# Short column ranges and full-width last row blocks in the small products of a linear-attention gradient

## The chip, the cores and the metric

The kernel runs on one core of a Trainium2 chip. A core has TensorE (matrix products; PE in the profile, PEld for the loading of its stationary operand), VectorE (DVE), ScalarE (ACT), GpSimd (POOL) and SyncE (SP, which here only issues transfers), an on-chip memory of 128 partitions (SBUF), and eight accumulation banks (PSUM) that TensorE writes and VectorE and ScalarE read. Transfers between memories (DMA) are issued on the queues of SP, ACT and POOL.

The metric is the device time of one execution in microseconds (us). The kernel before took 1066.45 us, the median of three runs (1065.12, 1066.45, 1068.38).

## The reference

Two attention blocks are computed, forward and backward, on 2048 tokens of width 448 with 16 heads of 28 columns. Block A is linear attention, block B is softmax attention with one shared key and value head. The program returns the output and the gradients of both inputs and of all weights.

```python
# block A (x: 2048 x 448, wqkv: 448 x 1344, wo: 448 x 448)
q, k, v = heads of x @ wqkv                      # 16 heads of 28 columns
phi = lambda t: where(t > 0, t + 1, exp(t)) + 1e-6
pq, pk = phi(q), phi(k)
kv  = einsum("bhsd,bhse->bhde", pk, v)           # one 28 x 28 matrix per head
z   = einsum("bhsd->bhd", pk)
num = einsum("bhqd,bhde->bhqe", pq, kv)
den = einsum("bhqd,bhd->bhq", pq, z) + 1e-6
a   = concat_heads(num / den) @ wo
# block B: softmax((x wq)(x wk)^T / sqrt(28)) (x wv), then @ wo
# result: [a, b] and the vector-Jacobian product with grad_out for all eight inputs
```

What matters for this document is `kv`. Laid out for all heads at once it is a 448 x 448 matrix in which only 16 blocks of 28 x 28 on the diagonal are not zero. Its transpose, its gradient and the transpose of that have the same shape.

## The kernel before

The work has two halves. Block A and the preparation of block B (`phase_A`, `phase_B_pre`) come first and take about 218 us. Then one loop over 512 steps computes the softmax attention of block B and its gradients, in an order that is written out by hand (`tc.manual_schedule()`). The change lies in the first half only. There, a scheduler in the framework puts each engine's instructions in order at build time; each engine then runs its own list in that order, and waits between engines are semaphores. Every transfer on the SP and ACT queues also uses one of eight completion semaphores in turn, so that its issue waits until the transfer that had the same semaphore before has landed.

Matrices of width 448 are held as four chunks of 128, 128, 128 and 64 rows (`DC_ROWS`, line 19). A product with 448 output rows is thus done in four row blocks `i`, each summing over four chunks `k` of the contraction. `HR` (line 22) gives for each chunk the columns in which a block-diagonal matrix is not zero: 140, 168, 140 and 84 columns, where neighbours overlap by 28 because heads straddle the chunk borders.

These parts of block A are touched, in their order of execution:

- `blkprod` (lines 285 to 297) makes a block-diagonal matrix: for each row block it multiplies only the columns of `HR[i]` and masks the result on VectorE (line 297). It is used four times: for the transpose of kv (line 333), for kv (line 336), for the transpose of its gradient (line 428) and for its gradient (line 453). Each has 32 products, 8 of them in the last row block.
- `prod_to` (lines 299 to 306) makes a product of two 448 x 448 matrices, one of them block-diagonal. With `full=False` the block-diagonal one is the stationary operand and only the chunks that are not zero are summed (`chunks_of`): KO (line 341) and VWT (line 451), 10 products each. With `full=True` the block-diagonal one is the moving operand, and all its 448 columns are streamed for each of 16 products: KOT (line 339) and VW (line 429). The result is copied out of PSUM by whichever of ScalarE and VectorE the scheduler picks (line 306).
- The last loop of weight gradients (lines 457 to 477) makes, for each row block `i`, two results. The first is K1, held in two parts of bfloat16, times the gradient of kv, which is block-diagonal: 8 products of 448 columns (line 463). The second is kv times the two parts of G: 4 or 6 products of 512 columns (line 473). ScalarE copies each result into a tile `osb` (lines 466 and 476) and issues its store (lines 467 and 477). There are three `osb` tiles and four PSUM tiles named `agen`.

All of these products go through `mm` (line 80), so that their line in the profile is L81. In the last row block, `i = 3`, the stationary operand has 64 columns instead of 128.

Around these parts stand large products on the same engine: `st1`, `st3`, `outA` and the sums into `gacc` (lines 347 to 388), the weight gradients `gw` (lines 409 to 426, called on lines 430 and 504), the loop that makes `gkn` (lines 431 to 437) and the loop that makes the input gradient (lines 509 to 516).

Of the kernel before, what the change touches and what calls it, by code (L numbers as in the profile page):

```python
# [11 lines left out]
BF16 = mybir.dt.bfloat16  # L12
# [4 lines left out]
D = 448  # L17
P = 128
# [3 lines left out]
HR = [(0, 140), (112, 280), (252, 392), (364, 448)]  # L22
# [3 lines left out]
def kernel(  # L26
# [21 lines left out]
    nc = tc.nc  # L48
# [31 lines left out]
    def mm(out_ap, lhsT, rhs, start=True, stop=True):  # L80
        nc.tensor.matmul(out_ap, lhsT=lhsT, rhs=rhs, start=start, stop=stop, tile_position=(0, 0))  # L81
# [23 lines left out]
    def w_T(t, w, off, r3=0):  # L105
        for cc in range(4):
            r = DC_ROWS[cc]
            r0 = r3 if cc == 3 else 0
            nc.sync.dma_start_transpose(t[:, :, cc * P:cc * P + r], w[r0:r0 + r, cc, off:off + 512])
        return t  # L110
# [6 lines left out]
    def chunks_of(i):  # L117
        lo, hi = HR[i]
        return [k for k in range(4) if k * P < hi and k * P + DC_ROWS[k] > lo]

    def cs(i):
        return slice(i * P, i * P + DC_ROWS[i])

    def phase_A(pa, cA, cB, awk, psA):
# [11 lines left out]
        w3 = R3  # L136
# [24 lines left out]
        woA = cA.tile([P, 4, 512], BF16, name="woA")  # L161
# [33 lines left out]
        def mask(i):  # L195
            lo, hi = HR[i]
            return blkm[:, i, :, :].rearrange("p h e -> p (h e)")[0:DC_ROWS[i], 0:hi - lo]

        K1T = [ppB[:, 8 + 4 * i:12 + 4 * i, :] for i in range(2)]
        K1 = [cA.tile([P, 4, 4, P], BF16, name=f"K1{i}") for i in range(2)]  # L200
        kv_blk, kvT_blk, KO, KOT = (cA.tile([P, 4, D], BF16, name=n) for n in ("kv", "kvT", "KO", "KOT"))
        dkv_blk = R4[:, :, 0:D]
        dkvT_blk, VW, VWT = kvT_blk, KOT, KO
        zrow = cA.tile([P, D], BF16, name="zrow")
# [9 lines left out]
        for t in (KO, KOT):  # L214
            nc.gpsimd.memset(t[64:128, 3, :], 0.0)
        zero = [t[:, c, :] for t in (kvT_blk, kv_blk, dkv_blk) for c in range(4)]
        wvT = w_T(cA.tile([P, 4, D], BF16, name="wvT"), w3, 2 * D)
        woT = w_T(cA.tile([P, 4, D], BF16, name="woT"), woA, 0)

        def xT(st):  # L220
            ps = gen([P, 4, P], BF16)
# [63 lines left out]
        def blkprod(dst, lhs, rhs, name="agen"):  # L285
            for i in range(4):
                lo, hi = HR[i]
                r = DC_ROWS[i]
                ps = psA.tile([P, D], F32, name=name)
                ops = [(l_, r_) for l_ in lhs for r_ in rhs]  # L290
                n = len(ops) * 4
                k = 0
                for l_, r_ in ops:
                    for c in range(4):
                        mm(ps[0:r, 0:hi - lo], l_(c, i)[:, 0:r], r_(c)[:, lo:hi], start=(k == 0), stop=(k == n - 1))
                        k += 1
                nc.vector.tensor_tensor(out=dst[0:r, i, lo:hi], in0=ps[0:r, 0:hi - lo], in1=mask(i), op=ALU.mult)

        def prod_to(dst, lhs, rhs, full):
            for i in range(4):  # L300
                r = DC_ROWS[i]
                ps = gen([P, D])
                ks = range(4) if full else chunks_of(i)
                for n, k in enumerate(ks):
                    mm(ps[0:r, :], lhs[:, k, cs(i)], rhs[:, k, 0:D], start=(n == 0), stop=(n == len(ks) - 1))
                nc.any.tensor_copy(out=dst[0:r, i, :], in_=ps[0:r, :])

        def den(q4):
# [81 lines left out]
        GT = [gaB[:, 4 * i:4 * i + 4, :] for i in range(2)]  # L390
        G = [v4(ga[:, 4 * i:4 * i + 4, :]) for i in range(2)]
# [33 lines left out]
                g_ = nc.gpsimd.dma_start(out_2[c * P:c * P + r, blk * D:(blk + 1) * D], sb[0:r, :])  # L425
            return g_

        blkprod(dkvT_blk, [lambda c, i: woT[:, c, cs(i)]], [lambda c: GT[0][:, c, 0:D], lambda c: GT[1][:, c, 0:D]])
        prod_to(VW, wvT, dkvT_blk, True)
        gw(gqn, 0)  # L430
        for st in range(NS):
            ps = gen([P, D])
# [17 lines left out]
            nc.sync.dma_start(wo_pr[32 * j + 1:32 * j + 1 + DH, g, 0:D], B_wo[h * DH:(h + 1) * DH, :])  # L450
        prod_to(VWT, dkvT_blk, wvT, False)
        nc.gpsimd.dma_start(VWT[64:128, 3, :], wqT[0:64, 3, :])
        blkprod(dkv_blk, [lambda c, i: GT[0][:, c, cs(i)], lambda c, i: GT[1][:, c, cs(i)]], [lambda c: woT[:, c, :]])
        gkT = v4(gaB)
        for q4 in range(4):
            dma_T(gkT, gkn, 4 * q4, 4)
        for i in range(4):
            r = DC_ROWS[i]
            ps = gen([P, D])
            n = 0  # L460
            for j in range(2):
                for k in range(4):
                    mm(ps[0:r, :], K1[j][:, i, k, 0:r], dkv_blk[:, k, :], start=(n == 0), stop=(n == 7))
                    n += 1
            sb = awk.tile([P, 512], BF16, name="osb")[:, 0:D]
            nc.scalar.activation(out=sb[0:r, :], in_=ps[0:r, :], func=ACT.Copy)
            nc.scalar.dma_start(out_2[i * P:i * P + r, 2 * D:3 * D], sb[0:r, :])
            ps = gen([P, 512])
            ks = chunks_of(i)
            n = 0  # L470
            for j in range(2):
                for k in ks:
                    mm(ps[0:r, :], kv_blk[:, k, cs(i)], G[j][:, :, k, :], start=(n == 0), stop=(n == 2 * len(ks) - 1))
                    n += 1
            sb = awk.tile([P, 512], BF16, name="osb")[:, 0:D]
            nc.scalar.activation(out=sb[0:r, :], in_=ps[0:r, 0:D], func=ACT.Copy)
            nc.scalar.dma_start(out_3[i * P:i * P + r, :], sb[0:r, :])
# [31 lines left out]
        for st in range(NS):  # L509
            ps = gen([P, D])  # L510
            n = 0
# [607 lines left out]
```

## Time and profile before

| | |
|---|---|
| median of the runs | 1066.45 us (1065.12 to 1068.38) |
| span of the profiled execution | 1064.7 us |
| TensorE busy | 1023.1 us, 96%, 16241 products |
| VectorE, ScalarE, GpSimd busy | 899.5, 870.4, 780.7 us |
| first product of the hand-ordered loop | 217.9 us after the start |
| KOT, start of its products to start of the next | 52.99 to 56.23 us |
| VW, the same | 105.97 to 109.21 us |
| last loop of weight gradients | 135.19 to 145.79 us |

The span runs from the first to the last instruction; the page gives no other time for the profiled execution, and the three runs lie 0.4 to 3.7 us above the span. Busy time of TensorE counts a product from its start to its modelled end, and products overlap, so that the distance between starts is what one costs in a row of them. A line of the timeline gives start, length, engine, source line, operation, the tile written and the tiles read, the shape, the count, and in brackets the idle time before it with what ended it. A line of the chain gives start, length and what the program's end is traced back to.

### The profile page before, as it was taken

What the parts mean: (1) busy time and instruction counts of PE and PEld (TensorE: products, weight loads), DVE (VectorE), ACT (ScalarE), POOL (GpSimd) and SP (SyncE); (2) the same over time, 40 slices, a digit from 0 to 9 for tenths busy, and PEclk for the clock granted to TensorE, in tenths of its full rate; (3) what the DMA queues carried; (4) which work ended last, traced back from release to release, by engine and by line L of the source; (5) the groups of instructions that cost most, each with busy time, mean ns of one, the idle gap of its engine ahead of it and who ended that gap; (6) DMA issues with size and microseconds to landing.
All of it is one profiled execution on the core that took longest, in us unless ns stands there. A gap on an engine that the chain in (4) does not pass through costs nothing.

```text
span 1064.7 us, 40036 instructions
## 1 busy us (share of the span) xinstructions
PE 1023.1 (96%) x16241; PEld 489.1 (46%) x16241; DVE 899.5 (84%) x1797; ACT 870.4 (82%) x1741; POOL 780.7 (73%) x1033
## 2 busy tenths in 40 slices
PE   9999999998999999999999999999999999999998
PEld 5555455434444444444444444444444444444444
DVE  7887400459999999999999999999999999999942
ACT  6463222489999999999999999999999999999522
POOL 6001242218888898899889989988998999888881
PEclk9999999999999999999999999999999999999999
DMA  9849899079999999999999999999999999999963
GB/s 264 167 108 192 171 203 246 22 137 181 193 188 196 182 203 189 188 202 191 197 181 197 181 196 195 193 189 194 196 197 192 199 190 183 208 190 177 222 141 89
DMA packets 689937, 195.15 MB, mean 183 GB/s; under 512 B 670616, under 2 KB 687792, under 8 KB 689752
## 3 DMA queue, kind: packets, MB, share of 16 engines
q1 hardware_dynamic: 680152, 179.92, 99.6%
q0 software_dynamic: 4640, 8.71, 2.9%
q10 hardware_dynamic: 4960, 3.96, 1.3%
q8 instruction: 127, 2.08, 0.8%
q14 instruction: 58, 0.48, 0.2%
HBM read 12.60 MB, written 10.84 MB: 22 GB/s over the span
## 4 chain that ended last, share of the span: by engine, by line
PE 43%; ACT 32%; issue 14%; POOL 5%; DVE 4%; DMA 1%; ACTq 0%; DVEq 0%; POOLq 0%
ACT cp L938 16%; PE agen L81 14%; ACT eT L970 13%; PE agen L656 10%; PE aacc L656 10%; PE aacc L81 5%; POOL dsT L939 3%; PE aacc L790 2%; ACT eT L924 2%; PE aacc L821 1%; DVE dsT L936 1%; DVE dsx L1003 1%; DMA out_dram<-dsT 1%; POOL eT L754 1%; POOL out_dram L778 0%
## 5 line engine op out<-in xcount | busy, mean ns | idle before, releaser
L939 POOL TENSOR_TENSOR dsT<-cp,eT 128x512 bf16<-128x512 bf16 x512 | 587.9, 1156 | 78.9 <-ACT cp L938 71.7
L1003 DVE STREAM_TRANSPOSE dsx<-dsT 128x512 f32<-128x512 f32 x512 | 357.6, 699 | 2.9 <-POOL dsT L939 0.8
L656 PEld LDWEIGHTS <-R 32*128 32x128 bf16 (+1 forms) x9104 | 227.9, 94 | 274.1 <-issue 238.4
L936 DVE TENSOR_TENSOR dsT<-agen,eT 128x512 bf16<-128x512 f32 x512 | 341.7, 667 | 10.9 <-PE agen L656 5.6
L938 ACT ACTIVATE cp<-agen 128x512 bf16<-128x512 f32 x512 | 315.8, 617 | 12.3 <-PE agen L656 11.2
L924 ACT ACTIVATE eT<-aacc 128x512 bf16<-128x512 f32 x512 | 313.6, 612 | 14.8 <-PE agen L656 4.8
L970 ACT ACTIVATE eT<-aacc 128x512 bf16<-128x512 f32 x512 | 322.2, 629 | 0.0
L656 PE MATMUL agen<-dsx,qX 32*32 32x512 bf16 x4096 | 267.6, 375 | 0.0
L656 PE MATMUL agen<-doT,R 32*128 32x256 bf16 x2048 | 247.1, 269 | 3.4 <-DVE dsT L936 1.4
L656 PE MATMUL aacc<-R,R 32*128 32x256 bf16 (+1 forms) x2240 | 218.2, 268 | 7.2 <-DVE oTs L800 2.5
L656 PE MATMUL agen<-eT,R 128*32 128x256 bf16 x2048 | 157.5, 274 | 0.1
L656 PE MATMUL agen<-dsT,R 128*32 128x256 bf16 x2048 | 156.8, 274 | 0.1
L656 PEld LDWEIGHTS <-qX 32*32 32x32 bf16 x4096 | 79.8, 89 | 113.7 <-issue 53.3
L656 PE MATMUL aacc<-eN,don 128*32 128x512 bf16 x1024 | 97.1, 379 | 0.1
L81 PEld LDWEIGHTS <-R 128*128 128x128 bf16 (+1 forms) x517 | 40.8, 98 | 43.5 <-issue 11.5
L406 POOL COPY pk<-R 128x256 bf16<-128x256 bf16 x4 | 1.6, 397 | 73.8 <-DVE R L366 73.7
L81 PE MATMUL agen<-R,R 128*128 128x448 bf16 (+1 forms) x180 | 42.1, 361 | 0.6 <-ACT R L225 0.6
L832 POOL COPY qst<-R 128x512 bf16<-128x512 bf16 x56 | 34.2, 611 | 4.0 <-DMA qX<-qst 3.9
L656 PEld LDWEIGHTS <-don 128*32 128x32 bf16 x1024 | 33.8, 97 | 1.4 <-issue 1.0
L804 POOL TENSOR_TENSOR prod<-R,oTs 128x128 f32<-128x128 bf16 x64 | 27.6, 431 | 9.3 <-DVE oTs L800 9.3
L422 DVE TENSOR_TENSOR osb<-aacc,pr 64x448 bf16<-64x448 f32 x2 | 1.2, 618 | 38.3 <-DMA out_dram<-osb 24.4
L955 DVE TENSOR_SCALAR R<-agen 64x256 bf16<-64x256 f32 x64 | 27.3, 427 | 3.6 <-PE agen L656 1.6
(231 smaller groups left out, 967.8 us busy)
## 6 DMA issues: line engine op xcount, KB each, us to landing
out_dram<-osb ACTq DMA_DIRECT2D x22, 112.0 KB
eN<-eT SPq DMA_TRANSPOSE x128
xa<-in_A_x_dram SPq DMA_DIRECT2D x8, 224.0 KB
ga<-in_grad_out_dram SPq DMA_DIRECT2D x4, 448.0 KB
xa<-in_grad_out_dram POOLq DMA_DIRECT2D x4, 448.0 KB, 6.1
out_dram<-wdq POOLq DMA_DIRECT2D x8, 224.0 KB, 4.0
eT<-in_grad_out_dram SPq DMA_DIRECT2D x4, 448.0 KB
eT<-in_B_x_dram SPq DMA_DIRECT2D x4, 448.0 KB
```

The costliest lines, as they stand in the source:

```text
L81: nc.tensor.matmul(out_ap, lhsT=lhsT, rhs=rhs, start=start, stop=stop, tile_position=(0, 0))
L656: nc.tensor.matmul(out, lhsT=lhsT, rhs=rhs, start=start, stop=stop, tile_position=pos, skip_group_check=True)
L790: nc.tensor.transpose(onp[:, qb, :, :].rearrange("p h c -> p (h c)"), oTs[0:64, qb * P:(qb + 1) * P], identF[0:64, 0:64], tile_position=(0 ...
L804: nc.gpsimd.tensor_tensor(out=prod[b][:], in0=dnv, in1=os_, op=ALU.mult)
L832: eng.tensor_copy(out=st.rearrange("p (b s) a j -> p b s a j", s=2)[:, :, s, :, :], in_=src.unsqueeze(2).to_broadcast([P, 4, 4, 32]))
L924: nc.scalar.activation(out=eT(u)[:, 0, :], in_=sp[0][:, :], func=ACT.Exp, scale=scale)
L936: nc.vector.tensor_tensor(out=dst[:, 0, :], in0=dp[0][:, :], in1=ew[:, 0, :], op=ALU.mult)
L938: nc.scalar.activation(out=cp[:, :], in_=dp[1][:, :], func=ACT.Copy)
L939: nc.gpsimd.tensor_tensor(out=dst[:, 1, :], in0=cp[:, :], in1=ew[:, 1, :], op=ALU.mult)
L955: nc.vector.tensor_scalar(out=qT_B[g][64 * hp:64 * hp + 64, qc * 256:(qc + 1) * 256], in0=oq[64:128, 0:256], scalar1=scale, scalar2=None, ...
L970: nc.scalar.activation(out=eT(u)[:, 1, :], in_=sp[1][:, :], func=ACT.Exp, scale=scale)
L1003: nc.vector.transpose(out=dsx[b][:, tp, :, :, :].rearrange("p h t c -> p (h t c)").bitcast(F32), in_=dsT[y][:, :, :].rearrange("p h c -> p ...
```

## The change

Three things are edited.

First, the products whose moving operand is block-diagonal stream, for each chunk, only the columns of `HR`. This holds for KOT and VW (`prod_to` with `full=True`) and for K1 times the gradient of kv. A new helper, `by_heads`, issues them: 140, 168, 140 or 84 columns each, written to the same columns of one PSUM bank; only the first product of a group starts the sum.

Second, the last row block is computed 128 rows wide in all of these products, with 128 stationary columns; rows 64 to 127 of the result are not read.

Third, to have 64 more columns to read behind the last chunk, `wvT`, `woT`, `kv_blk` and `kvT_blk` become parts of one tile `blks` with 64 zero columns at its end; `cols` gives a row block of 128 columns that runs on into the chunk behind it.

```diff
-        kv_blk, kvT_blk, KO, KOT = (cA.tile([P, 4, D], BF16, name=n) for n in ("kv", "kvT", "KO", "KOT"))
+        KO, KOT = (cA.tile([P, 4, D], BF16, name=n) for n in ("KO", "KOT"))
+        blks = cA.tile([P, 16 * D + 64], BF16, name="blks")
+        nc.gpsimd.memset(blks[:, 16 * D:], 0.0)
+        wvT_, woT_, kv_blk, kvT_blk = (blks[:, 4 * D * n:4 * D * n + 4 * D].rearrange("p (c d) -> p c d", d=D) for n in range(4))
+        blk_at = {id(t): 4 * n for n, t in enumerate((wvT_, woT_, kv_blk, kvT_blk))}
...
-        wvT = w_T(cA.tile([P, 4, D], BF16, name="wvT"), w3, 2 * D)
-        woT = w_T(cA.tile([P, 4, D], BF16, name="woT"), woA, 0)
+        wvT = w_T(wvT_, w3, 2 * D)
+        woT = w_T(woT_, woA, 0)
...
-                        mm(ps[0:r, 0:hi - lo], l_(c, i)[:, 0:r], r_(c)[:, lo:hi], start=(k == 0), stop=(k == n - 1))
+                        mm(ps[:, 0:hi - lo], l_(c, i), r_(c)[:, lo:hi], start=(k == 0), stop=(k == n - 1))
...
+        def cols(t, k, i):
+            if id(t) in blk_at:
+                return blks[:, (blk_at[id(t)] + k) * D + i * P:(blk_at[id(t)] + k) * D + (i + 1) * P]
+            return t[:, k, i * P:(i + 1) * P]
+
+        def by_heads(ps, pairs):
+            n = 4 * len(pairs)
+            for m in range(n):
+                lhs, rhs = pairs[m // 4]
+                lo, hi = HR[m % 4]
+                nc.tensor.matmul(ps[:, lo:hi], lhsT=lhs(m % 4), rhs=rhs[:, m % 4, lo:hi], start=(m == 0), stop=(m == n - 1),
+                                 tile_position=(0, 0), skip_group_check=True)
 
         def prod_to(dst, lhs, rhs, full):
             for i in range(4):
                 r = DC_ROWS[i]
                 ps = gen([P, D])
-                ks = range(4) if full else chunks_of(i)
-                for n, k in enumerate(ks):
-                    mm(ps[0:r, :], lhs[:, k, cs(i)], rhs[:, k, 0:D], start=(n == 0), stop=(n == len(ks) - 1))
+                if full:
+                    by_heads(ps, [(lambda k: cols(lhs, k, i), rhs)])
+                else:
+                    ks = chunks_of(i)
+                    for n, k in enumerate(ks):
+                        mm(ps[:, :], cols(lhs, k, i), rhs[:, k, 0:D], start=(n == 0), stop=(n == len(ks) - 1))
                 nc.any.tensor_copy(out=dst[0:r, i, :], in_=ps[0:r, :])
...
-        blkprod(dkvT_blk, [lambda c, i: woT[:, c, cs(i)]], [lambda c: GT[0][:, c, 0:D], lambda c: GT[1][:, c, 0:D]])
+        blkprod(dkvT_blk, [lambda c, i: cols(woT, c, i)], [lambda c: GT[0][:, c, 0:D], lambda c: GT[1][:, c, 0:D]])
...
-            n = 0
-            for j in range(2):
-                for k in range(4):
-                    mm(ps[0:r, :], K1[j][:, i, k, 0:r], dkv_blk[:, k, :], start=(n == 0), stop=(n == 7))
-                    n += 1
+            by_heads(ps, [(lambda k: K1[0][:, i, k, :], dkv_blk), (lambda k: K1[1][:, i, k, :], dkv_blk)])
...
-                    mm(ps[0:r, :], kv_blk[:, k, cs(i)], G[j][:, :, k, :], start=(n == 0), stop=(n == 2 * len(ks) - 1))
+                    mm(ps[:, :], cols(kv_blk, k, i), G[j][:, :, k, :], start=(n == 0), stop=(n == 2 * len(ks) - 1))
```

More of the change, by code (lines that the diff above doesn't have):

```diff
@@ L452, in phase_A @@
         nc.gpsimd.dma_start(VWT[64:128, 3, :], wqT[0:64, 3, :])
-        blkprod(dkv_blk, [lambda c, i: GT[0][:, c, cs(i)], lambda c, i: GT[1][:, c, cs(i)]], [lambda c: woT[:, c, :]])
+        blkprod(dkv_blk, [lambda c, i: cols(GT[0], c, i), lambda c, i: cols(GT[1], c, i)], [lambda c: woT[:, c, :]])
         gkT = v4(gaB)
```

## The prediction

> **What bounds the kernel now.** I read the page first, then the chain that ended last over the first 250 us, then the timeline of TensorE, VectorE and ScalarE around the changed products, then the transfers there. The page:
>
> ```profile
> span 1064.7 us, 40036 instructions
> PE 1023.1 (96%) x16241; PEld 489.1 (46%) x16241; DVE 899.5 (84%) x1797; ACT 870.4 (82%) x1741; POOL 780.7 (73%) x1033
> PEclk9999999999999999999999999999999999999999
> ```
>
> TensorE is busy nearly always and its clock is full in every slice. Busy time alone proves nothing, so the chain has to say whether a shorter product moves the end. From its answers for 42 to 104 us and 125 to 250 us:
>
> ```profile
> 50.52 2.13 PE aacc L81 x32
> 52.65 7.79 PE agen L81 x66
> ...
> 69.35 0.76 PE agen L81 x4
> ...
> 124.93 20.92 PE agen L81 x127
> 145.86 9.19 PE aacc L81 x48
> 155.04 1.64 PE aacc L85 x16
> 156.68 44.55 PE agen L81 x224
> ```
>
> All three places of the change (KOT, VW and the last loop of weight gradients) lie on unbroken stretches of TensorE. Four products of 448 columns take 0.76 us, so 189 ns from start to start. Until 217.9 us almost everything is such a chain; what TensorE saves there, the start of the hand-ordered loop can gain.
>
> **The price of a short product.** The timeline of TensorE and of its loads has a row of just such products, the 32 of kv (140, 168, 140 and 84 columns), beside KOT and VW:
>
> ```profile
> 50.52 2.13 PE L81 MATMUL aacc<-R,pqpT 128*128 128x140 bf16 x32 [0.56 <-DVE kvT L297]
> 52.58 0.56 PE L81 MATMUL agen<-Zm,R 128*128 128x16 bf16 x16
> 52.99 3.30 PE L81 MATMUL agen<-kvT,woA 128*128 128x448 bf16 x16
> ...
> 52.58 0.47 PEld L81 LDWEIGHTS <-R 128*128 128x128 bf16 x16
> ...
> 105.97 3.31 PE L81 MATMUL agen<-kvT,wvT 128*128 128x448 bf16 x16
> ```
>
> kv goes from 50.52 to the next group at 52.58: 2.06 us for 32, or 64 ns each, weight loads and row-block switches included. KOT and VW have the same mix of widths (133 columns on average), so I take 64 ns for `by_heads`. Loads do not hold it up: the 16 loads at 52.58 end 0.47 us later, and with 98 ns for the last they start 25 ns apart.
>
> [...]
>
> **KOT.** From 52.99 to the next group at 56.23 is 3.24 us for 16; at 64 ns it is 1.03, so 2.2 us of TensorE go. Next late is VectorE, which is nearly full here: its sums of `st1` at 61.82 (line 353) come behind 16 multiplications of `den_rx`. It idled 0.72 us for the first KOT copy and 0.39 us for KO, and both idles go, 1.1 us. For the other 1.1 us the build order of the changed kernel has TensorE do five more of the 64 sums into `gacc` (189 ns each, 0.95 us) before the first transpose, so they are missing at the end of that stage, where VectorE has idles of 0.4 to 1.0 us per step and can keep up. KOT's copies (two on ScalarE, two on VectorE, 0.54 us each) may hold back KO by some 0.4 us, less than KO's slack now. Bounds 1.1 (only VectorE's idle) to 2.2; I take 2.0, because the work moved is still done.
>
> **VW.** 3.24 us become 1.03: 2.2 us. Its operand is masked by 106.1 us, about when the fourth product now needs it, one filler of 189 ns is put in front, and 41 products of `gw` stand behind it, so its four copies stay hidden. GpSimd's clearing of `wo_pr` (line 447), the SP loads behind that (line 450) and the `gkn` loop wait for the end of `gw` and move with it. Bounds 1.7 (a wait of one copy, 0.54 us, for a PSUM tile) to 2.2; I take 2.15.
>
> **The last loop of weight gradients.** TensorE and ScalarE, from the timeline:
>
> ```profile
> 135.19 1.69 PE L81 MATMUL agen<-R,K 128*128 128x448 bf16 x8
> 136.72 1.03 PE L81 MATMUL agen<-ga,kv 128*128 128x512 bf16 x4
> ...
> 144.83 1.03 PE L81 MATMUL agen<-ga,kv 128*64 128x512 bf16 x4
> 145.79 0.55 PE L81 MATMUL aacc<-wdq,xa 128*128 128x448 bf16 x2
> ...
> 136.97 0.54 ACT L466 ACTIVATE osb<-agen 128x448 bf16<-128x448 f32 x1 [3.71 <-PE agen L81]
> 139.36 0.34 ACTq L467 DMA_DIRECT2D out_dram<-osb  x1
> 139.80 0.54 ACT L476 ACTIVATE osb<-agen 128x448 bf16<-128x448 f32 x1 [2.29 <-DMA R<-in_B_wo_dram]
> ...
> 142.99 0.54 ACT L476 ACTIVATE osb<-agen 128x448 bf16<-128x448 f32 x1 [1.54 <-DMA out_dram<-osb]
> ```
>
> The loop lasts 10.60 us: 32 products of 448 columns at 190 ns (6.09) and 20 of 512 at 216 ns (4.31), with two small gaps. With 64 ns the 32 take 2.06, so TensorE alone needs 6.4 us and would save 4.2. But ScalarE is already late. Its first copy ends at 137.51, yet its store is issued at 139.36, because the store's completion semaphore belongs to an SP load still on its way; the second copy stands behind it. The fourth copy then waits for an `osb` tile, until the first store lands, 3.6 us after its issue. The eighth result needs the PSUM tile that this fourth copy frees, and `gw` and all else on TensorE is queued behind it. Now this costs nothing; with the short products it decides.
>
> In the built list of instructions with their waits, the changed kernel's first store takes its semaphore after the transfer issued just before that load, the fourth transpose of B_x (SP, ended its issue at 134.79). Counted from the loop's start, it can land between 2.0 us (the transfers' rate falls to 105 GB/s at 137 us, 23 at 138) and 4.1 (the load behind it, 139.3); I take 3.3. The store lands 2.2 (GpSimd's smaller stores of `osb` between 100 and 222 us) to 3.6 us after; I take 3.4, nearest to the row here. Then the fourth copy, 0.54, and the eighth result, 4 times 0.216: 3.3 + 3.4 + 0.55 + 0.87 = 8.1 us, 2.5 us less than 10.6. Bounds: 4.1 + 3.6 + 0.55 + 0.87 = 9.1, so 1.5; and TensorE's own 4.2. Copies five to eight drain beside `gw`, 10.8 us long, before the next `agen` tile is wanted.
>
> **128-wide last row blocks.** A row block with 64 columns costs a gap at its start: 0.10 us at 143.29, where six products of 216 ns from 141.90 end at 143.19. KO takes 2.10 us for 10 (1.89 at 189 ns). Six groups outside the parts above (four `blkprod`, KO, VWT) at 0.1 us give 0.6 us. Against it, 84 columns under a 128-column load could cost more than under a 64-column one; the loads' 25 ns are below the 35 ns that 84 columns take at the 448-column rate. Bounds 0 and 1.2 (twice the gap, as KO has); I take 0.6.
>
> **The rest.** The new memset of 64 columns is one more GpSimd instruction among those of the first 20 us, before any product reads it: nothing. Columns read from the neighbouring chunk were written at least one stage earlier: no new wait. The transposes of `gkn` (SP, issued until 148.7) are wanted from 157.9 us by 16 steps of 2.1 us; seven us earlier they still are there. The order of SP, ACT and POOL is otherwise the same but for a few swaps.
>
> **The sum.** 2.0 + 2.15 + 2.5 + 0.6 = 7.2 us, with ends of 4.3 and 9.8. The profiled execution's span of 1064.7 becomes 1057.5; the page has no other time for it, and the median of the runs is 1.75 above, so 1059.2 us.
>
> **Rivals.** *The evacuation takes most of it:* KOT at 1.1, the loop at 1.5, VW 1.7, wide rows 0: 4.3 us, 1062.2 us. For it speak VectorE's full stretch from 53 to 64 us and ScalarE's waits above; against it the fillers.
>
> *The gain is swallowed at the entry of the hand-ordered loop* (1066 us): some transfer, not TensorE, would have to set its start. The chain has a load of `wo` there (2.95 us at 217.89), but it is issued right behind TensorE's last preparation and moves with it; the last transposes of `xa` are issued by 182 us, 36 us ahead. So little speaks for it.
>
> *Slower:* products of `by_heads` add into columns that the product before them wrote a moment ago, overlapping by 28. If each had to wait for the one before to end, a 448-column product's length of 352 ns against 189 from start to start gives 163 ns on top of 64: 227 ns, 64 times 25 ns more than now's 202, so 1.6 us more for TensorE. It decides from 202 ns on, and in full (352 ns, no overlap at all) it is 9.6 us slower, 1076 us. Against it: the row of kv adds into the very same columns at 64 ns.
>
> **How the numbers follow.** The likeliest case, 5 to 10 us saved, has 0.70; the evacuation case, 3.2 to 5 us, 0.13; swallowed 0.10; slower 0.07. What a measurement here can tell from no change is 0.3%, 3.2 us, so faster has 0.83, same 0.10, slower 0.07. The range goes from 10.4 us saved (the end of 9.8 and the scatter of the runs) to 2.9: 1056.0 to 1063.6.
>
> **What would show it.** KOT and VW each about 1.0 us long; the `gkn` loop starting near 114.4 instead of 118.9 us; the last loop of weight gradients 8 us long, with a wait of TensorE for ScalarE's line of the kv copy before its eighth result; the first product of the hand-ordered loop near 210.7 instead of 217.9 us; 846.8 us from there to the end as before. Products of `by_heads` well over 64 ns apart, a loop of 9 us or more, or a hand-ordered loop of another length would make it wrong.

## The result, and the profile after

The changed kernel takes 1064.88 us, the median of 13 runs (1061.81 to 1066.89), against 1066.45 us for 13 runs of the kernel before beside it. The ratio is 0.9976, with a 95% interval of 0.9966 to 0.9987: about 1.6 us by the medians and 2.6 us by the ratio, less than the 0.3% that the prediction named as the bound. The forecast was 1059.2 us, with a range from 1056.0 to 1063.6. The time lies above the range, by 1.3 us.

The profiled execution has a span of 1063.9 us, against 1064.7. Two lines of its page:

```profile
span 1063.9 us, 40030 instructions
...
PE 1013.7 (95%) x16232; PEld 487.2 (46%) x16241; DVE 899.6 (85%) x1799; ACT 869.6 (82%) x1739; POOL 781.7 (73%) x1034
```

TensorE has 9.4 us less to do (1023.1 before), and the span has hardly moved. So TensorE waits where it did not wait before. The page can't say where; the timeline can.

**The short products are as short as predicted.** The timeline of TensorE after, at KOT and in the last loop of weight gradients:

```profile
52.95 1.09 PE L313 MATMUL agen<-blks,woA 128*128 128x140 bf16 x16
53.96 0.55 PE L81 MATMUL agen<-Zm,R 128*128 128x16 bf16 x16
...
138.17 0.63 PE L313 MATMUL agen<-R,K 128*128 128x140 bf16 x8
138.63 1.46 PE L81 MATMUL agen<-ga,blks 128*128 128x512 bf16 x6
```

KOT goes from 52.95 to 53.96 us: 1.01 us for 16 products, 63 ns each, where it took 3.24. VW's last 15 products, from 103.25 to 104.17, take 61 ns each. In the last loop eight products take 0.46 us, 58 ns each, where 448 columns took 190 ns.

**The gain arrives at the `gkn` loop, and goes there.** The first product of that loop stood at 118.89 us before. The timeline after:

```profile
113.66 3.20 PE L81 MATMUL agen<-KOT,R 128*128 128x448 bf16 x16
122.30 10.84 PE L81 MATMUL agen<-KOT,R 128*128 128x448 bf16 x48 [5.44 <-DVE wdq L457]
132.97 2.06 PE L81 MATMUL agen<-blks 128*128 128x448 bf16 x10
```

The loop starts 5.23 us earlier than before, more than was forecast. Then TensorE does 16 products, has filled its four PSUM tiles, and waits 5.44 us for VectorE. The chain that ended last says what VectorE waits for; its columns are start, length and what it was traced back to:

```profile
114.61 0.37 SPq L109
...
115.03 2.37 DMA ga<-R
...
117.68 0.02 POOL ga L422
...
118.25 2.77 DMA out_dram<-osb
...
121.10 0.62 DVE osb L442
121.72 0.54 DVE wdq L457
122.30 10.20 PE agen L81 x45
132.50 6.52 DMA pk<-in_B_x_dram
...
139.09 2.82 DMA out_dram<-osb
```

Read downwards: a transpose that SP issues at 115.03, as soon as it is done with the one ahead of it (`ga<-R`, the last part of `wkT`), lands at 117.40. Behind it GpSimd clears rows of `wkT` (line 422). Behind the clearing, in GpSimd's queue, stand the stores of the first `gw` (line 445). The first of them frees one of the three `osb` tiles at 121.02, VectorE can then write the fourth row block into it (line 442), and only behind that instruction does VectorE's work of the `gkn` loop begin (line 457). GpSimd's timeline before, and then after, shows the turn:

```profile
116.46 0.47 POOL L402 MEMSET ga<- 64x448 bf16 x1 [10.51 <-DMA ga<-R]
117.83 1.64 POOL L425 DMA_DIRECT2D out_dram<-osb  x3 [0.90 <-ACT osb L424]
119.50 1.81 POOL L447 MEMSET R<- 128x2048 bf16 x1
```

```profile
117.68 0.47 POOL L422 MEMSET ga<- 64x448 bf16 x1 [14.40 <-DMA ga<-R]
118.25 1.64 POOL L445 DMA_DIRECT2D out_dram<-osb  x3
119.93 1.81 POOL L467 MEMSET R<- 128x2048 bf16 x1
```

Before, the clearing ended 0.9 us ahead of the stores, and the stores waited for ScalarE's copies, which begin at 116.99. After, ScalarE's copies begin at 111.75, but the clearing has not become earlier: it ends at 118.15. The same wait of GpSimd for `ga<-R` was in the trace of before, with 0.9 us to spare. What sets it is SP's queue; before, and then after:

```profile
106.93 4.89 SPq L396 DMA_TRANSPOSE ga<-gaT  x2
111.90 3.13 SPq L109 DMA_TRANSPOSE ga<-R  x2
```

```profile
107.41 6.19 SPq L416 DMA_TRANSPOSE ga<-gaT  x2
113.69 2.57 SPq L109 DMA_TRANSPOSE ga<-R  x2
```

SP issues one transpose behind the other, each some 1.2 to 3.8 us long. This row does not follow TensorE; it is even 1.8 us later.

**Then the clock halves.** The trace after in stretches of 2 us; the columns are the stretch and its length, busy time (and instructions) of PE, PEld, DVE, ACT and POOL, the granted TensorE clock, the share of the DMA engines and GB/s:

```profile
118.00:120.00 2.00, 0.00 (x0) 0.00 (x0) 0.00 (x0) 0.00 (x0) 1.86 (x5) 1.00 1.14 212
...
122.00:124.00 2.00, 1.70 (x5) 0.69 (x5) 2.00 (x6) 0.00 (x0) 0.55 (x1) 0.54 0.25 66
124.00:126.00 2.00, 2.00 (x8) 0.81 (x7) 1.64 (x5) 0.00 (x0) 0.00 (x0) 0.61 0.65 136
126.00:128.00 2.00, 2.00 (x12) 1.05 (x11) 1.74 (x6) 0.00 (x0) 0.00 (x0) 1.00 0.82 177
```

After the idle time TensorE gets 0.54 and 0.61 of its clock, and works on 5 and 8 products in 2 us, against 12 in the row behind them. By these rows that is about 0.46 x 1.70 + 0.39 x 2.00 = 1.56 us lost. The account of the `gkn` loop: 12.12 us long before (118.89 to 131.01), 19.31 after, which is 5.44 of wait, 1.56 of clock and 0.19 of rest more.

The slow stretch is 3.41 us long in this trace, from 122.16 to 125.57 us at a granted clock of 0.50, and begins within the 5.44 us of idle time, 0.14 us before its end. The other executions of this document with such a wait are in the last section.

**The last loop.** It starts at 136.72 us, 1.53 later than before, and ends at 143.45, 2.34 earlier: 6.73 us long in place of 10.60. TensorE and ScalarE there:

```profile
136.72 0.48 PE L313 MATMUL agen<-R,K 128*128 128x140 bf16 x3
...
142.59 1.02 PE L81 MATMUL agen<-ga,blks 128*128 128x512 bf16 x4 [0.28 <-ACT osb L492]
143.45 2.81 PE L81 MATMUL aacc<-wdq,xa 128*128 128x448 bf16 x14
```

```profile
139.09 0.35 ACTq L483 DMA_DIRECT2D out_dram<-osb  x1
139.55 0.55 ACT L492 ACTIVATE osb<-agen 128x448 bf16<-128x448 f32 x1 [1.24 <-DMA pk<-in_B_x_dram]
```

The first product of the hand-ordered loop comes at 215.54 us (217.89 before), 72.1 us behind the end of the last loop as before. From there to the end it is 848.4 us (846.8), so that the span shows 0.8 us of the 2.35. The other 1.6 us go in the hand-ordered loop of this one execution; over all sixteen profiled executions of this document that stretch takes 844.6 to 848.4 us.

### The profile page after: what moved, and what is told of

It is laid out like the page before. It is cut to its first block, busy times and chain, and to the rows that moved or that the text cites. A ratio compares the mean times of both kernels' runs of the same rounds, so it can differ in the third digit from the quotient of the medians.

```text
span 1063.9 us, 40030 instructions
## 1 busy us (share of the span) xinstructions
PE 1013.7 (95%) x16232; PEld 487.2 (46%) x16241; DVE 899.6 (85%) x1799; ACT 869.6 (82%) x1739; POOL 781.7 (73%) x1034
## 4 chain that ended last, share of the span: by engine, by line
PE 44%; ACT 32%; issue 13%; DVE 4%; POOL 4%; DMA 2%; ACTq 0%; DVEq 0%; SPq 0%; POOLq 0%
ACT cp L954 16%; ACT eT L986 13%; PE agen L81 12%; PE agen L672 11%; PE aacc L672 10%; PE aacc L81 7%; POOL dsT L955 3%; PE aacc L806 2%; ACT eT L940 2%; PE aacc L837 1%; DVE dsx L1019 1%; DVE dsT L952 1%; DMA dsx<-R 1%; DMA pk<-in_B_x_dram 1%; DMA out_dram<-osb 1%
## 5 line engine op out<-in xcount | busy, mean ns | idle before, releaser
L81 PEld LDWEIGHTS <-R 128*128 128x128 bf16 x517 | 41.3, 99 | 50.2 <-issue 19.3
```

## The experiments

Two theories stood at the start. Theory A: the only thing in the way is the fourth row block's wait for an `osb` tile. Theory B: the place in GpSimd's queue is in the way; the late clearing holds the stores, and behind them the clearing of `wo_pr` (line 467), SP's loads of `wo` (line 470) and, since the last loop's stores use completion semaphores of SP's loads, that loop too. Rival C, for the last loop: its stores bound it, however short its products are.

Times are medians, ratios are against runs of the kernel before beside them (medians of 1066.3 to 1067.1 us). The table at the end has the places in the traces.

**The fourth row block in a tile of its own**

```diff
-                sb = awk.tile([P, 512], BF16, name="osb")[:, 0:D]
+                sb = mrow if c == 3 and blk == 0 else awk.tile([P, 512], BF16, name="osb")[:, 0:D]
```

> The changed kernel, with the last row block of the first weight gradient (`gw(gqn, 0)`) written to an unused part of `mrow` instead of an `osb` tile. VectorE then no longer waits for the first store to free a tile. Theory A (that tile wait alone cost the gain): VectorE's sum follows ScalarE's copy at about 114.4 us, TensorE's 5.4 us wait and its slow clock behind it go, the last loop of weight gradients starts near 129.7 and ends near 137.5 us, the hand-ordered loop starts near 209.5 instead of 215.6 us, and the run is 5 to 6 us faster than the changed kernel. Theory B (the cause is the place in GpSimd's queue: the memset that waits for a transposition holds up not only the store but also the clearing of `wo_pr`, with it SP's loads, and with those the completion semaphores of the stores in the last loop): the last loop starts near 130 but still ends at 140.5 to 143.4 us, the hand-ordered loop starts at 212.6 to 215.5, and the run is 0 to 3 us faster than the changed kernel.

1064.51 us (11 runs), ratio 0.9979 (0.9963 to 0.9996): the same as the changed kernel. By the medians that is 0.4 us below the changed kernel, where theory B gave 0 to 3 and theory A 5 to 6. The 5.4 us wait is gone, and TensorE waits in the last loop instead. Its timeline, TensorE and then ScalarE:

```profile
139.97 2.58 PE L81 MATMUL agen<-ga,blks 128*128 128x512 bf16 x6 [4.71 <-ACT osb L492]
```

```profile
138.93 0.34 ACTq L483 DMA_DIRECT2D out_dram<-osb  x1
139.37 0.55 ACT L492 ACTIVATE osb<-agen 128x448 bf16<-128x448 f32 x1 [6.35 <-DMA pk<-in_B_x_dram]
```

The first store is issued at 138.93 us, where it stands with (139.09) and without the cure, and ScalarE's second copy stands behind it. Theory A falls: the gain got through one gate and was lost at the next.

**The clearing of `wkT`'s rows behind that of `wo_pr` in GpSimd's queue**

```diff
-        for t in (wqT, wkT):
-            nc.gpsimd.memset(t[64:128, 3, :], 0.0)
+        nc.gpsimd.memset(wqT[64:128, 3, :], 0.0)
...
-        nc.gpsimd.memset(wo_pr, 0.0)
+        z_ = nc.gpsimd.memset(wo_pr, 0.0)
+        with tc.issue_after(z_.ins):
+            nc.gpsimd.memset(wkT[64:128, 3, :], 0.0)
```

> The changed kernel, with the memset of rows 64 to 127 of `wkT` put behind the clearing of `wo_pr` in GpSimd's queue. Theory A: the first store goes out near 112.4 us and lands near 115.3, so TensorE waits about 1 us instead of 5.4 at full clock, the last loop of weight gradients starts near 130.7 and ends near 138.5, the hand-ordered loop starts near 210.5. Theory B: the same start, but its end follows SP, whose loads start near 118.4 instead of 121.8 us (behind its own transpositions): 139.5 to 140.5 us, and the hand-ordered loop starts at 211.6 to 212.6. Both: 3 to 5 us faster than the changed kernel.

1063.18 us (11 runs), ratio 0.9962 (0.995 to 0.9975). The stores go out at 111.84 us, and the wait shrinks to 0.30. In the last loop the first store is issued at 134.98, and 2.86 us of waiting are left. Hand-ordered loop from 210.75 us, where the prediction had it. By its places this execution fits theory A (a last loop that ends near 138.5 and a hand-ordered loop near 210.5), but the time is only 1.7 us below that of the changed kernel, where 3 to 5 were expected. The span of this execution, 1057.3 us, lies 5.9 us below the median of the timed runs, where that of the kernel with both cures lies 1.9 below, so its wait in the last loop may be shorter than the usual one.

**Both cures**

> The changed kernel with both edits: own tile, and memset behind the clearing of `wo_pr`. Theory A: no wait of TensorE between 113 and 130 us, the hand-ordered loop starts near 209.5 us. Theory B: the same as with the memset alone within 0.7 us, 211 to 212.5 us, because SP's loads set the end of the last loop of weight gradients.

1062.48 us (6 runs), ratio 0.9955 (0.994 to 0.997). No wait in the `gkn` loop, but 3.90 us in the last loop with half the clock behind it (0.50 from 138 to 140 us). The hand-ordered loop starts at 213.11 us, 3.6 us later than theory A says and 0.6 later than theory B does. ScalarE there:

```profile
135.64 0.37 ACTq L484 DMA_DIRECT2D out_dram<-osb  x1
136.11 0.55 ACT L493 ACTIVATE osb<-agen 128x448 bf16<-128x448 f32 x1 [5.54 <-DMA pk<-in_B_x_dram]
```

In the kernels whose last loop stores from ScalarE the first store follows SP's first load of `wo` by 16.5 to 18.3 us, wherever TensorE is (table). The landing that the store waits for is that of SP's fourth transposition of B_x. It overwrites `pk`, which VectorE reads in the `gkn` loop; where the last loop starts on time (own tile, late clearing, both cures, SP's order in the table), VectorE has read the last of `pk` 4.4 to 7.9 us before that transposition starts, which is 0.09 us behind the end of SP's instruction ahead of it, so SP's row holds it and not the `gkn` loop. (After the change alone it starts 0.03 us behind that read, and the two can't be told apart.) So SP's queue sets the last loop as well, and a cure at the `gkn` loop alone ends in the next wait.

**Only the last loop short; KOT and VW with 448 columns**

> The changed kernel with full 448-column streams in KOT and VW again; only K1 times the gradient of kv is short, and all last row blocks are 128 wide. Theories A and B alike: the first weight gradient ends near 118.3 us, GpSimd's memset is done before it, TensorE does not wait behind it, the last loop of weight gradients starts near 134.6 and is 6.7 to 8 us long, the hand-ordered loop starts at 213.4 to 214.7 us, so it is as fast as the whole change or 1 us faster. Rival C (the stores bound the last loop whatever its products): it ends near 145 us and the hand-ordered loop starts near 217.3.

1065.56 us (12 runs), ratio 0.9986 (0.9977 to 0.9996). I expected no wait in the `gkn` loop, and there are 3.23 us, although the loop starts no earlier than before (119.11 us). GpSimd's clearing stands at 120.93 in this build. So the wait needs no faster TensorE, only a later SP; the 0.9 us to spare of before are what that build's row of transposes gave. This run says nothing on rival C, since the loop starts so late (140.05) that its store has little left to wait.

**The last loop's stores issued by GpSimd, with both cures**

```diff
-            nc.scalar.dma_start(out_2[i * P:i * P + r, 2 * D:3 * D], sb[0:r, :])
+            nc.gpsimd.dma_start(out_2[i * P:i * P + r, 2 * D:3 * D], sb[0:r, :])
...
-            nc.scalar.dma_start(out_3[i * P:i * P + r, :], sb[0:r, :])
+            nc.gpsimd.dma_start(out_3[i * P:i * P + r, :], sb[0:r, :])
```

> The changed kernel with both cures (the clearing of wkT's rows behind that of wo_pr, the fourth row block of the first gw in a tile of its own), and besides the last loop's eight stores issued by GpSimd in place of ScalarE. Theory B with its second place: in the two-cure kernel the first store, standing in ScalarE's queue, waits for an SP transfer's semaphore (issued 136 us), and TensorE idles 3.9 us for the fourth copy. With the stores in another queue ScalarE's copies follow TensorE; the loop from 129.0 us takes 6.4 to 7.3 us, the hand-ordered loop starts near 208 us (72.1 us behind the loop's end, as in all runs so far), 1056 to 1058.5 us in all. Rival D: the three osb tiles and the landing of a store (3.4 us), not the place in ScalarE's queue, bound the loop: TensorE's wait of 3 to 4 us stays, now on VectorE's or ScalarE's copy behind a GpSimd store, the loop takes 9 us or more, 1061 to 1063 us.

1057.72 us (6 runs), ratio 0.9913 (0.9893 to 0.9932): faster than both kernels. TensorE and GpSimd in the last loop:

```profile
137.50 1.02 PE L81 MATMUL agen<-ga,blks 128*128 128x512 bf16 x4 [1.10 <-ACT osb L493]
```

```profile
132.69 0.56 POOL L484 DMA_DIRECT2D out_dram<-osb  x1 [4.03 <-ACT osb L483]
```

The store goes 0.3 us behind its copy. The loop is 7.56 us long; the expected 6.4 to 7.3 was a little too good, since the three `osb` tiles still cost 1.1 us, so rival D has a part in it. Rival C falls: the same eight stores are made, and the loop is 3 us shorter than before. The hand-ordered loop starts at 210.68 us and not near 208; 1.4 us of that went near 50 us (last section). A second measurement of this kernel, beside two others below:

> The kernel with all three cures once more, on the same chip as the two others of this call: 1056.5 to 1059 us.

It gave 1057.68 us (6 runs), ratio 0.9927 (0.9911 to 0.9943).

**The stores alone**

> The changed kernel with one edit: the last loop's eight stores issued by GpSimd. The two waits are in series: as the loop starts late (136.7 us, behind the 5.4 us wait in the gkn loop), its first store has only 1.2 us left to wait, and the loop is already 6.7 us long. Theory B: this edit alone gives at most 0.3 us, 1064.2 to 1065.2 us, hand-ordered loop near 215.3 us. If the stores' place were worth something by itself (the second place independent of the first), 1061 to 1063 us.

1064.26 us (12 runs), ratio 0.998 (0.9961 to 0.9999); the wait in the `gkn` loop is 4.96 us. The two places are in series: opening the second alone gives nothing.

**The cures without the change**

The kernel before with both cures, and with all three:

> The kernel before with the two cures (late clearing of wkT's rows, own tile for the fourth row block). In the kernel before, the clearing ends 0.9 us before the first gw store is wanted, so theory B expects nothing from it: TensorE's end of the last loop stays within 0.7 us of 145.8, 1065.7 to 1066.9 us. Rival: the two cures are worth some 2 to 3 us by themselves and the gains of the cured kernels have little to do with the short products: 1063 to 1064.5 us.

> The kernel before with all three cures (late clearing of wkT's rows, own tile for the fourth row block, the last loop's stores issued by GpSimd). Theory B: before the change TensorE is the last to end in all three places, so the cures move nothing: 1065.0 to 1066.9 us, hand-ordered loop 217.4 to 218 us. Rival: the cures are a gain of their own of 3 us or more, and the changed kernel with the cures (1057.7 us) owes that much of its gain to them: 1062 to 1063.5 us.

1066.12 us, ratio 0.9989 (0.9976 to 1.0002), and 1066.04 us, ratio 0.9986 (0.9975 to 0.9996). The hand-ordered loop starts at 217.42 and 217.94 us (217.89 before). The cures by themselves are worth 1.5 us by the last ratio (0.4 to 2.7), and nothing of it is seen in the places of the traces. With the short products the same three cures reach 1057.7, some 8.3 us below 1066.04 (in another measurement, with the kernel before at 1067.06 and 1067.0).

**The parts alone**

KOT and VW short, the last loop with 448 columns; then the same with all three cures; then only the 128-wide row blocks and the common tile:

> The changed kernel with the last loop of weight gradients left at eight streams of 448 columns per result (its row blocks 128 wide); KOT and VW short as in the change. Theory B: the 4.4 us that KOT and VW save go in the wait behind GpSimd's clearing and in the slow clock behind it, so the loop starts at 136 to 137 us and lasts 10.4 to 10.6 us as before the change: hand-ordered loop 218.5 to 219.5 us, 1066.5 to 1068 us, no faster than the kernel before. Rival: the saving at KOT and VW is real at the end and the short last loop is what gives it back: 1061 to 1063 us.

> The changed kernel with all three cures, but the last loop left at streams of 448 columns: KOT, VW and the 128-wide row blocks alone, with their way to the end open. The sum in the prediction for these three is 2.0 + 2.15 + 0.6 = 4.75 us: hand-ordered loop near 213.1 us, 1061 to 1062.5 us. Theory B says this (the short last loop is then worth the rest, 3.5 to 4.5 us, up to 1057.7). If KOT's saving is lost on VectorE as in the evacuation rival, 1063 to 1064.5 us.

> The changed kernel with KOT, VW and the last loop left at streams of 448 columns: only the 128-wide last row blocks and the common tile of the four operands remain. The prediction gives the wide blocks 0.6 us (0 to 1.2). From the traces run so far the loops of KO, VWT and of the masked products are 0.1 to 0.25 us shorter each. Theory B: the part of this that lies ahead of GpSimd's clearing is swallowed when the clearing is late, as it was in the kernel with only the last loop short (3.2 us wait there): 1065.5 to 1068 us. Rival: no wait at all when nothing is shorter, and 0.6 us or more faster: 1064.8 to 1066 us, with no wait of TensorE over 0.5 us between 115 and 130 us.

KOT and VW without cures: 1067.53 us (12 runs), ratio 1.0008 (0.9993 to 1.0023), no gain at all. TensorE there:

```profile
124.07 2.40 PE L81 MATMUL agen<-KOT,R 128*128 128x448 bf16 x6 [5.64 <-DVE wdq L457]
```

With the cures: 1060.86 us (5 runs), ratio 0.9941 (0.9926 to 0.9957). That is 5.2 us below the kernel before with the same cures (1066.04, run beside it), where the prediction's sum for these parts is 4.75. The short last loop then gives the rest, from 1060.9 to 1057.7: 3.2 us by these medians, and 1.5 to 3.0 by the ratios of the two measurements with it, where theory B had 3.5 to 4.5 and the prediction 2.5.

The wide row blocks alone: 1066.97 us (11 runs), ratio 1.0008 (0.9994 to 1.0022). The `gkn` loop starts 1.25 us earlier (117.64), and then waits:

```profile
122.86 9.24 PE L81 MATMUL agen<-KOT,R 128*128 128x448 bf16 x48 [2.02 <-DVE wdq L455]
```

So 1.25 us are there in this execution, just above the prediction's 0 to 1.2, and are swallowed at the same place.

**SP's order alone**

What was open is whether SP's order of transposes makes the clearing late. The transposes of `wqT` and `wkT` are written ahead of those of G; in the built order SP's list alone differs, with the last two parts of `wkT` ahead of G's two transposes:

```diff
+        wqT, wkT = (w_T(flat(ga[:, 8 + 4 * i:12 + 4 * i, :])[:, 0:4 * D].rearrange("p (c d) -> p c d", d=D), w3, i * D)
+                    for i in range(2))
         for i in range(2):
             nc.sync.dma_start_transpose(G[i].rearrange("p c h k -> p (c h) k"), flat(GT[i]))
...
-        wqT, wkT = (w_T(flat(ga[:, 8 + 4 * i:12 + 4 * i, :])[:, 0:4 * D].rearrange("p (c d) -> p c d", d=D), w3, i * D)
-                    for i in range(2))
```

> The changed kernel with one edit in SP's queue alone: the last two transposes of wkT stand ahead of the two transposes of G, not behind them. If SP's order is what holds the clearing of wkT's rows, those two land near 109 us, the clearing is done before ScalarE's copies of the first gw (111.8 us), the three stores go at once, and TensorE's 5.4 us wait and its half clock go: gkn loop without a wait over 0.5 us. SP's queue as a whole is as long as before, so the first wo load comes at 117.5 to 120.5 us, the last loop's first store 17 to 18 us behind it, and TensorE waits 2 to 4 us in that loop, as in the kernel with both cures: 1062 to 1063.7 us. Rival: the clearing waits for something else (TensorE's reads of ga, GpSimd itself): the wait of 3 us or more stays, 1064 to 1066 us.

1063.61 us (12 runs), ratio 0.9977 (0.9963 to 0.999). Its timeline, in order of time, of GpSimd, TensorE, SP and ScalarE:

```profile
110.84 0.47 POOL L422 MEMSET ga<- 64x448 bf16 x1 [7.68 <-DMA ga<-R]
112.48 1.64 POOL L445 DMA_DIRECT2D out_dram<-osb  x3 [1.18 <-ACT osb L444]
...
117.74 9.24 PE L81 MATMUL agen<-KOT,R 128*128 128x448 bf16 x48 [0.99 <-DVE wdq L457]
...
121.34 1.80 SPq L470 DMA_DIRECT2D R<-in_B_wo_dram  x4
...
139.44 0.34 ACTq L483 DMA_DIRECT2D out_dram<-osb  x1
...
140.48 2.72 PE L81 MATMUL agen<-ga,blks 128*128 128x512 bf16 x6 [6.08 <-ACT osb L492]
```

The clearing is done before it is wanted, and the wait falls from 5.44 to 0.99 us: the cause is SP's order, and the rival falls. (I expected under 0.5; the first store, issued at 112.48, took 3.98 us to land here, against 2.77 after the change alone.) But SP's queue is no shorter. Its first load of `wo` comes at 121.34, the first store 18.1 us later, and TensorE loses 6.08 us in the last loop, more than I expected (2 to 4), with half the clock behind it (0.50 from 140 to 142 us). This execution was timed at 1065.90 us, 2.3 above the median of its kernel, so the wait may be longer than the usual one. With the stores moved to GpSimd as well:

> The kernel with wkT's transposes first, and the last loop's eight stores issued by GpSimd. If these two queues are all that stood between the change and its gain, no other cure is needed: the last loop takes 7 to 7.7 us with one wait of about 1 us, hand-ordered loop 208.5 to 211 us, 1056.5 to 1059 us, within 1 us of the kernel with three cures run beside it. If the late clearing has another cause, 1063 to 1065 us, as with the stores moved alone.

1058.75 us (6 runs), ratio 0.9933 (0.9914 to 0.9953); the last loop is 6.67 us long. Two edits, neither of them on the change's products, give most of what the change had to give, 1 us less than three cures. These two were not run on the kernel before.

| kernel | `gkn` loop from | wait in it | first load of `wo` | first store | last loop | hand-ordered loop from | median |
|---|---|---|---|---|---|---|---|
| before | 118.89 | none | 121.34 | 139.36 | 135.19 to 145.79 | 217.89 | 1066.45 |
| after | 113.66 | 5.44 | 121.77 | 139.09 | 136.72 to 143.45 | 215.54 | 1064.88 |
| own tile | 115.05 | 0.29 | 122.40 | 138.93 | 131.42 to 144.26 | 216.37 | 1064.51 |
| late clearing | 112.91 | 0.30 | 117.71 | 134.98 | 129.32 to 138.63 | 210.75 | 1063.18 |
| both cures | 113.12 | none | 118.65 | 135.64 | 128.98 to 140.85 | 213.11 | 1062.48 |
| three cures | 114.94 | none | 120.65 | 132.69 | 130.80 to 138.36 | 210.68 | 1057.72 |
| three cures, second measurement | 113.55 | none | 117.38 | 131.30 | 129.41 to 137.55 | 209.87 | 1057.68 |
| stores alone | 113.53 | 4.96 | 121.16 | 137.95 | 136.06 to 144.27 | 216.37 | 1064.26 |
| SP's order | 113.55 | 0.99 | 121.34 | 139.44 | 130.56 to 145.59 | 217.83 | 1063.61 |
| SP's order, stores | 112.69 | 1.37 | 120.66 | 131.97 | 130.08 to 136.75 | 208.86 | 1058.75 |
| last loop alone | 119.11 | 3.23 | 125.01 | 142.51 | 140.05 to 148.02 | 220.13 | 1065.56 |
| KOT and VW alone | 115.23 | 5.64 | 123.53 | 141.80 | 139.46 to 149.83 | 221.93 | 1067.53 |
| KOT and VW, three cures | 115.17 | none | 119.08 | 133.63 | 131.03 to 141.40 | 213.72 | 1060.86 |
| wide blocks alone | 117.64 | 2.02 | 122.93 | 140.66 | 135.68 to 146.06 | 218.17 | 1066.97 |
| before, both cures | 118.41 | none | 120.81 | 139.14 | 134.71 to 145.30 | 217.42 | 1066.12 |
| before, three cures | 118.92 | none | 121.33 | 137.83 | 135.22 to 145.81 | 217.94 | 1066.04 |

(The places are those of one execution each, in us, and from one to another the stretch behind them varies: from the hand-ordered loop's start to the end it is 844.6 to 848.4 us. Some of these executions are far from the median of their kernel: late clearing was timed 4.1 us below it, KOT and VW alone 2.9 us and SP's order 2.3 us above.)

## Why the prediction was wrong

- **The price of a short product** was right: 58 to 63 ns against 64. With that the "slower" rival falls, for which overlapping sums had to cost over 202 ns. (That bound took all 64 products at 202 ns; the 32 of the last loop cost 190 before, so it lies at 196.) Nor do the weight loads hold the products up: a load takes 98 ns in the rows, and products that each need a new one come every 58 to 63 ns, so the loads overlap.
- **KOT and VW** were right in size: 2.2 us each on TensorE, the `gkn` loop at 113.66 us where 114.4 was forecast, and 5.2 us in the time once the way is free, against 4.75 with the wide blocks. The evacuation rival, which left KOT 1.1 us and VW 1.7, did not come: the `gkn` loop starts 5.23 us earlier.
- **The step that failed** is the sentence in the part on VW that GpSimd's clearing of `wo_pr`, SP's loads behind it and the `gkn` loop "wait for the end of `gw` and move with it". They do wait for the end of `gw`, but also for something that doesn't move: ahead of them in GpSimd's queue stands the clearing of `wkT`'s rows, which waits for SP's transposes. The trace of before shows it, with 10.51 us of GpSimd's idle time put down to `ga<-R` and an end 0.9 us ahead of the stores. I named what waits for the end of `gw` and did not ask what else each of them waits for, and by how much it was early. The stores had 0.9 us to spare, and TensorE had some 0.7 more (its 17th product of the `gkn` loop needs a PSUM tile at 121.93 us before, and VectorE's first instruction of that loop has freed one by 121.17), so at most about 1.6 of the 5.23 us could pass that gate. The experiment with SP's order alone shows that this is the cause.
- **The clock** is a term that the sum did not have: 1.56 us behind the wait of 5.44 us, by the rows at 0.54 and 0.61. Wait and clock take 7.0 us.
- **The last loop** was 6.73 us long where 8.1 was forecast, with the wait forecast for it, for the kv copy ahead of the eighth result, but only 0.28 us of it. This is not a better loop. The store's semaphore was put 3.3 us behind the loop's start (bounds 2.0 and 4.1), as if SP's row moved with TensorE. It did not: the fourth transposition of B_x, whose landing the store waits for, ended its issue at 134.99 us, against 134.79 before. It is tied to SP's queue: the store comes 16.5 to 18.3 us behind SP's first load. After, the loop starts late, so the store came 2.37 us behind its start. Where the loop starts on time, it came 5.7 to 8.9 us behind, and the loop lasts 9.3 to 15.0 us. The same wrong step was thus made twice, and the two waits lie in series: what the first doesn't take, the second does.
- **The wide row blocks** gave 1.25 us up to the `gkn` loop in one execution, forecast 0.6 (0 to 1.2) for all places: a little low.
- **The rival "swallowed"** had the right form, a transfer and not TensorE setting the start, with the wrong place: at the entry of the hand-ordered loop nothing was lost (72.1 us from the last loop's end to there, before and after). Its price of 1066 us was 1.1 us off. It had 0.10, because I looked for such a transfer in one place only.
- **The sum of 7.2 us** itself is about what the change can give: with the three cures the kernel is 0.73% to 0.87% below the kernel before (7.8 to 9.3 us), of which the cures alone make 1.5 us (0.4 to 2.7).

What stays open is why SP's row of transposes comes later in some builds: the last transpose of `wkT` starts at 113.2 us before, at 115.0 after and at 118.3 with the last loop alone. Between before and after the order among the other transposes differs, and so do the lengths of the single ones. Order is not all of it: with the last loop alone SP's order from 40 us on is that of before, and yet the row is 5 us late. What else makes it late was not found.

## What to carry to other kernels

When work on a full engine gets shorter, list every instruction that takes over its result, and for each the other things ahead of it in its own queue, with the time by which each was early before; along each path back to the full engine these margins add up (0.9 and 0.7 us here), and the path with the least to spare is what the change can gain until that one is moved too. A queue of transfers that runs back to back, as SP's did here (its last transpose of `wkT` started 1.8 us later where TensorE's `gkn` loop started 5.2 us earlier), has its own pace: loads, clearings and completion semaphores behind it need not move with the work that they serve. And when a cure of one wait changes nothing, look for the next wait in series before calling the cure useless: here the stores alone gave nothing, the late clearing alone 1.7 us by the medians, and all together 7.

## What was not expected of the hardware

Seven idle times of TensorE, of 3.23 to 6.08 us, each had at its end or behind it a stretch in which the granted clock was 0.50 or the products came about half as fast; those of 0.99 to 2.86 us in the same loops had none:

| kernel | idle time | at its end or behind it |
|---|---|---|
| after | 5.44 us | granted clock 0.50 from 122.16 to 125.57 us |
| stores alone | 4.96 us | 0.50 from 122 to 124 us |
| last loop alone | 3.23 us | 0.50 from 126 to 128 us |
| both cures | 3.90 us | 0.50 from 138 to 140 us |
| SP's order | 6.08 us | 0.50 from 140 to 142 us |
| own tile | 4.71 us | six products of 512 columns take 2.58 us (1.46 in the last loop after the change) |
| KOT and VW alone | 5.64 us | six products of 448 columns take 2.40 us (seven take 1.49 behind the 2.02 us of the wide blocks alone) |
| late clearing | 2.86 us | 1.00 from 136 to 140 us; six products of 512 columns take 1.46 us |

But near 50 us every one of these kernels, the one before too, has two short idle times of TensorE, 1.38 us and 0.56 to 0.58 us, and in five of the sixteen profiled executions the granted clock fell there too: it was 0.50 from 52 to 54 us in four (own tile, last loop alone, KOT and VW alone, three cures in the first measurement) and 0.71 on average from 50 to 54 us in the fifth (KOT and VW with three cures). In the other eleven it was 1.00 there. From the kernel with KOT and VW short and three cures:

```profile
50.70 2.87 PE L81 MATMUL aacc<-R,pqpT 128*128 128x140 bf16 x32 [0.57 <-DVE blks L301]
...
53.83 1.66 PE L313 MATMUL agen<-blks,woA 128*128 128x140 bf16 x16
55.33 0.55 PE L81 MATMUL agen<-Zm,R 128*128 128x16 bf16 x16
```

The same 16 products of KOT take 1.50 us there against 1.01, and what follows is 1.4 us late: the kernel with three cures starts its `gkn` loop at 114.94 us in the execution with the slow stretch and at 113.55 in the one without.

So the length of an idle time alone does not tell whether the clock falls: with nearly the same two idle times near 50 us it fell in five executions and not in eleven. What decides it is not shown here. The 1.4 us can be a part of the scatter of some 3 us between executions of one kernel; how much of it they make was not measured.
